# New job times and buffer letters for the first stage of a one-core S4 and gated-FFN kernel

## The chip, the core and the metric

One core of one Trainium2 chip runs the whole kernel. The metric is device microseconds (us) of one execution, the median of several runs. TensorE is PE in the profile (PEld its weight loads), VectorE is DVE, ScalarE is ACT, GpSimd is POOL, and SyncE is SP, which here only issues DMA transfers. "L843" is line 843 of the kernel.

## The reference

The input is `A_u`, 2048 tokens of 640 channels. A conditioning vector gives six rows that shift, scale and gate two residual blocks:

```python
mod = (_silu(c) @ w_mod).reshape(c.shape[0], 6, 1, -1)
sa, ca, ga, sb, cb, gb = (mod[:, 0], mod[:, 1], mod[:, 2], mod[:, 3], mod[:, 4], mod[:, 5])
h = _layernorm(x, axis=-1) * (1 + ca) + sa
x = x + ga * _A_ref(h, A_A_re, A_A_im, A_B_re, A_B_im, A_C_re, A_C_im, A_log_dt, A_Dskip)
h = _layernorm(x, axis=-1) * (1 + cb) + sb
x = x + gb * _B_ref(h, B_w_gate, B_w_up, B_w_down)
```

`_A_ref` builds for each channel a kernel of 2048 taps, `K = einsum("dn,dnl,dn->dl", Cc, exp(logdA * l), dB).real` over 192 complex modes, and convolves it with the tokens (written as an FFT of twice the length), plus a skip term. `_B_ref` is `((x w_gate) * (x w_up)) w_down` with 1536 hidden columns.

## The kernel before

The program has two stages. **The first stage** is block A. It works on five blocks of 128 channels (`db`) and interleaves two streams. One makes the taps K in 40 steps n of 16 channels each (8 steps a block): POOL multiplies out tables (`Ph`, `EQ`, `EP`, L732), ACT takes sines (tiles `tra`, `trb`), DVE multiplies both into the factors `QtA`, `PtA`, `QtB`, `PtB` (L787, L788, L793, L813), and PE sums them into the PSUM tile `kg`: 64 small matmuls at L828 (`kg_ma`, the A factors) and 64 at L843 (`kg_mb`, the B factors). ACT copies two steps' `kg` out as `Kt`. The other stream is the convolution by FFT, in jobs that are generators and advance one piece at a time: `u_k` (taps into the first FFT stage, PE L865), `u_pre` (tokens, PE L889), `u_g` and `u_c` (second stage, L913, product, and back, L973), and `u_d` (last stage, L996, and the residual, DVE L1002). `u_seeds` makes each block's seeds: PE transposes them at L538 to L540 into a PSUM bank, from which DVE reads several times, last at L609 into the tile `RH`. `u_stats` takes a tile's layer-norm statistics (DVE L487, L488).

The order on every engine's queue is that of one Python loop, which has 144 rounds t, three to a step n, each with two places `due(2 * t)` and `due(2 * t + 1)`. A table `SCHED` gives each piece of each job a number v; it runs at place `v // 10`, and within a place in the order of v. Negative numbers lie in the start, between pieces of the first seeds. Each engine works its queue strictly in that order. A second table, `SLOT`, gives the ring buffers: a string per ring, whose letters say which of two or three buffers the next tile takes. `psf` is a ring of three PSUM banks (`psfa`, `psfb`, `psfc`) that all the jobs share; a job that takes a bank waits until the last reader of that bank is done. `hf`, `gh`, `W`, `TV`, `xs` are rings in SBUF, in which loads also wait for the buffer's last reader.

```python
def due(x):
    for _, g in sorted(jobs.pop(x, []), key=lambda j: j[0]):
        next(g, None)
```

**The second stage** is block B in products of float32r halves; it starts at about 505 us (PE L1108) and its order is written out by hand.

The program is unrolled, so PE reads its instructions as a stream: its matmuls and weight loads come in by a DMA queue of their own ("q8 instruction" in the profile), in packets while it runs.

Of the kernel before, what the change touches and what calls it, by code (L numbers as in the profile page):

```python
# [69 lines left out]
    rstd=(142, 86),  # L70
    tab=(553, 739),
    fo=(149, 149, 202, 228),
    e0=(1, 159),
    ds=(339, 378, 319, 440),
    mc=((120, 175, 197, 201, 209), (192, 273, 273, 309, 317), (264, 369, 392)),
    q=(
# [4 lines left out]
    ),  # L81
    pre=(
# [5 lines left out]
    ),  # L88
    c=(
# [17 lines left out]
    ),  # L107
    k=(
        (402, 407),
        (224, 230),  # L110
        (454, 556),
        (421, 426),
        (484, 507),
        (517, 548),
        (639, 657),
        (603, 603),
        (706, 716),
        (664, 680),
        (777, 781),
        (803, 804),  # L120
        (1006, 1012),
        (1029, 1037),
        (1046, 1059),
        (1046, 1075),
        (1295, 1322),
        (1120, 1137),
        (1252, 1252),
        (1388, 1406),
        (1410, 1420),
        (1505, 1522),  # L130
        (1556, 1567),
        (1481, 1509),
        (1808, 1839),
        (1737, 1774),
        (1753, 1756),
        (1784, 1785),
        (1840, 1856),
        (1883, 1912),
        (1996, 2008),
        (2063, 2073),  # L140
        (2085, 2096),
        (2141, 2191),
        (2362, 2374),
        (2274, 2274),
        (2321, 2321),
        (2447, 2455),
        (2494, 2510),
        (2452, 2466),
    ),
    low=(167, 428, 668, 910, 1139, 1389, 1628, 1864, 2075),  # L150
    w=(2473, 2612, 2690, 2703, 2759, 2879),
    wl=(2602, 2481),
    wm=(2735, 2751),
    h=(2562, 2755, 2793, 2818, 2854, 2858, 2862, 2876),
    g=(
# [6 lines left out]
    xl=(2441, 2442),  # L162
# [3 lines left out]
    Kt="ababababababbabbaaba",  # L166
# [1743 lines left out]
```

## Time and profile before

| | |
|---|---|
| runs of before | 966.39, 969.98 and 972.0 us; median 969.98 |
| the profiled execution | 966.46 us, of which the span from first to last instruction is 964.6 |
| PE busy, 0 to 36 us | 17.7 of 36 (start) |
| PE busy, 36 to 505 us | 424.2 of 469 |
| PE busy, 505 us to the end | 455.4 of 459.6 (second stage) |
| transfers of PE's instructions | 91 packets, 1.49 MB |

An engine's idle time counts only where the others wait for it. A wait that the profile puts down to "issue" is one in which the engine waited for nothing that the profile shows as another engine or a data transfer.

### The profile page before, as it was taken

Reading aid. Unit: us, or ns where it says so; the run is one execution under the profiler, and the core shown is the slowest. Engines: PE = TensorE matmul, PEld = TensorE weight load, DVE = VectorE, ACT = ScalarE, POOL = GpSimd, SP = SyncE. Lnnn points to the kernel's source line nnn. Section 1 sums busy time; section 2 is a strip of 40 time slices with the busy share of each in tenths; the row PEclk is TensorE's granted clock in tenths of the full one; section 3 lists DMA queues with packets and bytes.
Section 4 is the critical chain, followed back from the end, with each engine's and each line's share of the span. In section 5 each row is a group of like instructions: output and inputs, shape, how many; then the busy total and the mean of one; then the engine's idle time right before and its main releaser. Section 6 shows DMA issues by size and latency. Waiting matters only on the chain.

```text
span 964.6 us, 27405 instructions
## 1 busy us (share of the span) xinstructions
PE 897.4 (93%) x11566; PEld 737.1 (76%) x11566; DVE 716.3 (74%) x1270; ACT 572.1 (59%) x996; POOL 471.1 (49%) x369
## 2 busy tenths in 40 slices
PE   2898888999899799999889999999999999999998
PEld 1675555788676478787648888889999788888998
DVE  8987898889889797876679555557575756578952
ACT  6899989787978868763356433344364543435430
POOL 3999996988499597650040445320113223231110
PEclk9997998999999799999999999999999999999999
DMA  7975674534376536457785675535546576758875
GB/s 237 333 235 174 198 224 157 169 110 149 88 218 188 145 92 193 131 189 249 248 268 197 211 245 161 196 137 151 192 150 190 156 245 213 247 164 290 246 242 191
DMA packets 156707, 188.56 MB, mean 195 GB/s; under 512 B 9764, under 2 KB 126376, under 8 KB 155432
## 3 DMA queue, kind: packets, MB, share of 16 engines
q1 hardware_dynamic: 147368, 155.47, 50.2%
q0 software_dynamic: 4752, 21.63, 7.7%
q10 hardware_dynamic: 4464, 9.70, 2.7%
q8 instruction: 91, 1.49, 0.7%
q14 instruction: 32, 0.26, 0.1%
HBM read 124.19 MB, written 62.59 MB: 194 GB/s over the span
## 4 chain that ended last, share of the span: by engine, by line
PE 70%; ACT 5%; DVE 5%; DMA 2%; issue 2%; POOL 0%; DVEq 0%; SPq 0%; POOLq 0%
PE pa L1108 20%; PE psg L1108 10%; PE pa L1545 7%; PE pa L1597 6%; PE kg L843 3%; PE psfc L973 3%; PE psfb L913 2%; PE kg L828 2%; PE psfb L973 2%; PE psfa L913 2%; PE psfc L913 2%; PE psg L1597 2%; PE psfc L889 1%; PE psfa L973 1%; PE psfb L889 1%
## 5 line engine op out<-in xcount | busy, mean ns | idle before, releaser
L1085 POOL TENSOR_TENSOR tf<-wur,wgb 128x256 f32<-128x256 f32 x23 | 17.6, 766 | 242.4 <-DVE wtl L1056 187.8
L732 POOL TENSOR_TENSOR EQ<-LQ,RH 128x1536 f32<-128x1536 f32 x40 | 114.7, 2867 | 10.7 <-DVE QtB L788 10.7
L1056 DVE TENSOR_TENSOR wtl<-tf,wth 128x256 fp32r<-128x256 f32 (+1 forms) x72 | 36.7, 512 | 59.1 <-ACT wth L237 59.1
L732 POOL TENSOR_TENSOR Phb<-LH,DH 128x1536 int32<-128x1536 int32 x21 | 59.6, 2837 | 39.0 <-ACT tra L237 32.6
L732 POOL TENSOR_TENSOR EP<-LP,RH 128x768 f32<-128x768 f32 x40 | 61.8, 1544 | 1.7 <-ACT RH L237 1.7
L1545 PE MATMUL pa<-wsg,sh 128*128 128x384 f32 (+1 forms) x304 | 58.1, 309 | 0.0
L732 POOL TENSOR_TENSOR Pha<-LH,DH 128x1536 int32<-128x1536 int32 (+1 forms) x20 | 54.0, 2702 | 5.3 <-ACT trb L237 4.4
L843 PEld LDWEIGHTS kg<-QtB,PtB 64*32 64x32 f32 x2560 | 39.6, 110 | 18.5 <-issue 13.4
L843 PE MATMUL kg<-QtB,PtB 64*32 64x64 f32 x2560 | 46.4, 222 | 6.0 <-issue 5.1
L1056 DVE TENSOR_TENSOR wsg<-wga,wsg 128x640 fp32r<-128x640 f32 x36 | 33.0, 918 | 17.0 <-ACT wsg L237 17.0
L1545 PEld LDWEIGHTS pa<-wsg,sh 128*128 128x128 f32 x304 | 45.4, 188 | 0.0
L1584 POOL DMA_DIRECT2D wsg<-wdc x21 | 11.2, 531 | 66.6 <-PE pa L1597 35.7
L237 ACT ACTIVATE sh<-a 128x512 fp32r<-128x512 f32 x55 | 33.3, 624 | 13.9 <-PE psg L1597 6.2
L237 ACT ACTIVATE wsg<-wga 128x640 fp32r<-128x640 f32 x36 | 26.3, 730 | 25.3 <-PE pa L1545 12.8
L1056 DVE TENSOR_TENSOR sl<-a,sh 128x512 fp32r<-128x512 f32 x55 | 38.0, 711 | 3.9 <-ACT sh L237 3.9
L1108 PE MATMUL pa<-hh,wsg 128*128 128x512 f32 x150 | 39.9, 393 | 0.0
L237 ACT ACTIVATE a<-pa 128x512 f32<-128x512 f32 x12 | 7.2, 596 | 49.5 <-PE pa L1108 49.5
L237 ACT ACTIVATE s<-pa 128x512 f32<-128x512 f32 x12 | 7.2, 598 | 47.9 <-PE pa L1108 47.9
L787 DVE TENSOR_TENSOR QtA<-trb,EQ 128x1024 f32<-128x1024 f32 x21 | 25.6, 1220 | 13.3 <-ACT trb L237 6.7
L237 ACT ACTIVATE wth<-tf 128x256 fp32r<-128x256 f32 (+1 forms) x72 | 32.4, 481 | 4.5 <-DVE tf L1086 1.8
L237 ACT ACT_TABLE_LOAD x25 | 32.1, 1283 | 4.4 <-DMA pta<-A_A_re 4.0
L1545 PE MATMUL pa<-wsg,sl 128*128 128x384 f32 (+1 forms) x152 | 34.5, 308 | 0.0
(647 smaller groups left out, 3216.6 us busy)
## 6 DMA issues: line engine op xcount, KB each, us to landing
wsg<-wdc POOLq DMA_DIRECT2D x21, 640.0 KB, 5.1
wgb<-B_w_gate SPq DMA_DIRECT2D x24, 320.0 KB, 3.3
wur<-B_w_up SPq DMA_DIRECT2D x24, 320.0 KB, 4.2
wsd<-wsg SPq DMA_DIRECT2D x12, 640.0 KB, 3.8
wga<-wdg SPq DMA_DIRECT2D x12, 640.0 KB, 5.4
wsg<-wsd POOLq DMA_DIRECT2D x12, 640.0 KB, 4.6
wdc<-xb SPq DMA_DIRECT2D x21, 320.0 KB, 6.5
TVa<-WD SPq DMA_DIRECT2D x20, 256.0 KB, 4.7
```

Source lines behind the costliest of these rows:

```text
L237: return S.activation(o, i, f, **kw)
L732: G.tensor_tensor(o.rearrange("p x (h l) -> p x h l", l=8), lo.unsqueeze(2).to_broadcast([P, rows, nh, 8]), hi.unsqueeze(3).to_broadcast([ ...
L787: return [lambda: V.tensor_tensor(Qt[:, :, :, 0:32], tr[:, :, :, ::-1], e[:, :, 0:32].unsqueeze(1).to_broadcast([P, 2, R, 32]), op=OP.mult ...
L828: PE.matmul(kg[j * 32 : j * 32 + 32, dd, :], PtA[:, c, dl * 4 + j, :], QtA[:, c, dl * 4 + j, :], start=dd == 0 and c == 0, stop=False, til ...
L843: PE.matmul(kg[j * 32 : j * 32 + 32, dd, :], PtB[lo : lo + 64, c, r, :], QtB[lo : lo + 64, c, r, :], start=False, stop=dd == 7 and c == 1, ...
L889: PE.matmul(r[c][o : o + 64], t_s1h[a, c] if i == 0 else t_one[a], h[a] if i == 0 else shr[a, d0].unsqueeze(1).to_broadcast([1, 4, P]), st ...
L913: PE.matmul(r[c][par * 64 : par * 64 + 64, i, :], t_tw[:, k0 + k, c, :], src[:, k, :], start=True, stop=True, tile_position=(0, par * 64))
L973: PE.matmul(r[par][:, i], t_ti[lo : lo + 64, qd * 4 + i, c, :], y[lo : lo + 64, i, :], start=k == 0, stop=k == len(x) - 1, tile_position=( ...
L1056: V.tensor_tensor(lo, v, hi, op=OP.subtract)
L1108: PE.matmul(ps, w[a][:, k], x[b][:, l], start=first and n == 0 and m == 0, stop=n == 2 and m == len(ks) - 1, skip_group_check=True)
L1545: PE.matmul(AC[tb][t][c], x[:, ts], w[:, cs], start=st, stop=f == NF - 1 and n == 2 and (c == 0 or t % 2 == 1))
L1597: PE.matmul(ps[t][:, :DC], AH[m][a][:, t * P : t * P + P], w[b], start=c == 0 and n == 0 and j in (0, 1, 3), stop=c == NH - 1 and n == 2, ...
```

## The change

Only numbers and letters in the two tables are new. The functions, the loop, the second stage and the number of matmuls, activations, vector operations and transfers are as before (on each engine the same instructions; the explicit semaphore waits between them differ by a few). Two lines of the diff stand for some 200:

```diff
-    ml=(38, 14, -923),
+    ml=(61, -905, -993),
...
-    psf="bacbaacbaacccabbcabcbacbbbcabcbcaabacabbbcbcbcabcaaacbbcbcabcababccabcabcacbacbbabacbacabcbabacbabcabcbbacbacbacbaccacba"
+    psf="cacbbcbbcbcabcabbcaabbabccbacabcbaccabababcacbcbabccabababcbcacabbcabcbacbacabbcbcabcbaacbacbacabbacbacbacbacbbcacbcbacb"
```

What it moves shows in the engines' orders. **First place**, some 310 us into the program of before, where the fourth block's seeds are made (n = 28 to 30). On PE, in before, from the second half of the transposes of seeds into `psfa` (`TVa`, `TVb` are loaded inputs of the last FFT stage, `Kta`, `Ktb` copied taps):

```order
L540 MATMUL psfa<-ct,prm 64x8x8
L996 MATMUL psfb<-TVa,ct 32x512 x4
L865 MATMUL psfa<-ct,Ktb 64x128 x8
L828 MATMUL kg<-QtA,PtAa 32x64 x32
L996 MATMUL psfc<-TVa,ct 32x512 x4
L996 MATMUL psfb<-TVb,ct 32x512 x4
L865 MATMUL psfc<-ct,Kta 64x128 x8
L843 MATMUL kg<-QtB,PtB 32x64 x32
```

and in the change:

```order
L540 MATMUL psfa<-ct,prm 64x8x8
L996 MATMUL psfb<-TVb,ct 32x512 x4
L996 MATMUL psfc<-TVa,ct 32x512 x4
L828 MATMUL kg<-QtA,PtAa 32x64 x32
L843 MATMUL kg<-QtB,PtB 32x64 x32
L865 MATMUL psfa<-ct,Ktb 64x128 x8
L913 MATMUL psfb<-f16b,t_tw 64x128 x2
```

The L865 that takes over bank `psfa` stood one row behind the L996 and now stands behind two of L996, L828 and L843; a third L996 has moved up to a place ahead of the L828 before these rows. On DVE at the same place, before, from the last cast of the seeds on:

```order
L598 CAST pta<-psfa 128x192
L1002 TENSOR_TENSOR xsa<-psfb,xsa 128x512
L609 TENSOR_TENSOR RH_153<-psfa,mults 128x1056
L609 TENSOR_TENSOR RH_151<-psfa,mults 128x1056
L619 TENSOR_SCALAR psfc<-ptb 128x192
```

and in the change:

```order
L598 CAST pta<-psfa 128x192
L813 TENSOR_TENSOR PtB<-trb,EP_142 128x512
L787 TENSOR_TENSOR QtB<-trb,EQ_140 128x16x32
L788 TENSOR_TENSOR QtB<-trb,EQ_140 128x16x32
L1002 TENSOR_TENSOR xsb<-psfb,xsb 128x512
L609 TENSOR_TENSOR RH_153<-psfa,mults 128x1056
L609 TENSOR_TENSOR RH_151<-psfa,mults 128x1056
L1002 TENSOR_TENSOR xsa<-psfc,xsa 128x512
L619 TENSOR_SCALAR psfb<-ptb 128x192
```

`PtB` and `QtB` of step n = 28, which L843 needs, now come ahead of both L609. On ACT at the same place, before, from the first sines of `trb` to the next `tra` (`RH`, `LQ`, `LP` are the seeds' exponentials):

```order
L237 ACTIVATE trb<-ab 128x512
L237 ACT_TABLE_LOAD
L237 ACTIVATE ptb<-ptb 128x192
...
L237 ACTIVATE RH_151<-RH_151 128x1056
L237 ACTIVATE PtAb<-Phb 128x1024
L237 ACT_TABLE_LOAD
L237 ACTIVATE tra<-Phb 128x512
L237 ACTIVATE tra<-PtAb 128x512
```

and in the change:

```order
L237 ACTIVATE trb<-ab 128x512
L237 ACTIVATE PtAb<-Phb 128x1024
L237 ACTIVATE tra<-Phb 128x512
L237 ACTIVATE tra<-PtAb 128x512
L237 ACT_TABLE_LOAD
L237 ACTIVATE ptb<-ptb 128x192
...
L237 ACTIVATE RH_151<-RH_151 128x1056
L237 ACT_TABLE_LOAD
L237 ACTIVATE trb<-Phb 128x512
L237 ACTIVATE trb<-PtAb 128x512
```

`PtAb` and both `tra` of step n = 29 have gone ahead of the six exponentials; `trb` stays behind them. On SP's queue, before, the transfers issued ahead of that place (`FH`, `WD`: intermediate FFT results in HBM; `gha`, `TVb`, `xsb` loads for later pieces):

```order
L900 DMA FH<-hfc 128x4x128
L903 DMA FH<-hfb 64x4x128 x2
L986 DMA TVb<-WD 128x4x128 x2
L991 DMA xsb<-A_u 128x4x128
L927 DMA gha<-FH 128x1024
L978 DMA WD<-Wa 128x1024
L900 DMA FH<-hfb 128x4x128
L903 DMA FH<-hfa 64x4x128 x2
```

and in the change:

```order
L900 DMA FH<-hfa 128x4x128
L903 DMA FH<-hfc 64x4x128 x2
L986 DMA TVb<-WD 128x4x128 x2
L991 DMA xsa<-A_u 128x4x128
L978 DMA WD<-Wb 128x1024
L900 DMA FH<-hfa 128x4x128
L903 DMA FH<-hfc 64x4x128 x2
L1008 DMA x2d<-xsa 128x4x128
```

The load of `gha` between the two groups of `FH` writes has gone to a later place. **Second place**, the start, on DVE at step n = 1 (`st` are layer-norm statistics of one tile), before:

```order
L1293 RECIPROCAL rs_94<-ry 128x10
L793 TENSOR_TENSOR PtAa<-trb,EP_143 128x1024
L487 BN_STATS st_533<-Wb 128x6 x2
L488 BN_AGGR mv_93<-st_533 128x2
L813 TENSOR_TENSOR PtB<-tra,EP_143 128x512
```

and in the change:

```order
L1293 RECIPROCAL rs_94<-ry 128x10
L487 BN_STATS st_501<-Wb 128x6 x2
L488 BN_AGGR mv_93<-st_501 128x2
L793 TENSOR_TENSOR PtAb<-trb,EP_143 128x1024
L487 BN_STATS st_506<-f16a 128x6 x2
L488 BN_AGGR mv_93<-st_506 128x2
L487 BN_STATS st_510<-f16a 128x6 x2
L488 BN_AGGR mv_93<-st_510 128x2
L487 BN_STATS st_534<-f16a 128x6 x2
L488 BN_AGGR mv_93<-st_534 128x2
L813 TENSOR_TENSOR PtB<-tra,EP_143 128x512
```

Four tiles' statistics now stand ahead of `PtB` of n = 1 where one did; before, the other three came right behind its `QtB`.

## Rows read from the trace of the kernel before

**Rows 1.** The page: busy time by engine, and PE's instruction queue (packets, MB, share).

```profile
PE 897.4 (93%) x11566; PEld 737.1 (76%) x11566; DVE 716.3 (74%) x1270; ACT 572.1 (59%) x996; POOL 471.1 (49%) x369
q8 instruction: 91, 1.49, 0.7%
```

**Rows 2.** Busy time by stretch: length, PE, PEld, DVE, ACT, POOL, clock, DMA share, GB/s.

```profile
60.00:160.00 100.00, 83.93 (x1762) 58.57 (x1762) 85.63 (x131) 92.69 (x156) 95.72 (x53) 0.92 0.66 215
160.00:310.00 150.00, 142.62 (x3342) 112.31 (x3343) 129.01 (x181) 121.80 (x206) 120.57 (x69) 0.98 0.48 143
310.00:335.00 25.00, 18.45 (x407) 13.22 (x406) 19.42 (x32) 20.45 (x31) 13.47 (x6) 0.80 0.51 149
335.00:441.00 106.00, 103.47 (x2584) 84.86 (x2582) 82.41 (x103) 75.35 (x131) 74.19 (x40) 1.00 0.53 160
```

**Rows 3.** PE's waits, 36 to 160 us: total, times, longest.

```profile
PE kg L843 <- issue: 2.2, 1, 2.2
...
PE psfb L865 <- issue: 1.0, 1, 1.0
...
PE psfc L390 <- issue: 0.8, 1, 0.8
```

**Rows 4.** PE's waits, 160 to 441 us.

```profile
PE psfa L865 <- DVE RH L609: 3.7, 1, 3.7
PE kg L843 <- issue: 2.8, 1, 2.8
PE kg L828 <- issue: 1.4, 2, 0.9
...
PE psfc L913 <- issue: 0.5, 1, 0.5
...
PE kg L832 <- issue: 0.4, 1, 0.4
```

**Rows 5.** Timeline of PE, 309 to 337 us: start, length, instruction, [idle before].

```profile
313.18 0.98 PE L843 MATMUL kg<-QtB,PtB 64*32 64x64 f32 x54
317.01 0.38 PE L843 MATMUL kg<-QtB,PtB 64*32 64x64 f32 x10 [2.85 <-issue]
...
318.68 1.93 PE L996 MATMUL psfb<-TVa,ct 64*32 64x512 f32 x8
...
335.50 1.10 PE L828 MATMUL kg<-QtA,PtAb 128*32 128x64 f32 x64 [0.23 <-DVE PtAb L793]
```

**Rows 6.** Queues at work from 310.3 to 314.4 us: packets, MB, share.

```profile
q1 hardware_dynamic: 718, 1.19, 90.5%
```

**Rows 7.** The same from 314.4 to 315.6 us.

```profile
q8 instruction: 1, 0.02, 4.9%
```

**Rows 8.** Transfers issued from 302 to 313 us: KB each, us to landing.

```profile
gha<-FH SPq DMA_DIRECT2D x1, 512.0 KB, 6.4
WD<-Wa SPq DMA_DIRECT2D x1, 512.0 KB
```

**Rows 9.** Timeline of DVE, 316 to 337 us.

```profile
318.80 0.37 DVE L595 CAST psfc<-psfa 128x192 int32<-128x192 f32 x1 [3.85 <-PE psfa L540]
...
334.22 1.22 DVE L793 TENSOR_TENSOR PtAb<-trb,EP 128x1024 f32<-128x1024 f32 x1
```

**Rows 10.** Timeline of ACT, 305 to 342 us.

```profile
317.42 0.60 ACT L237 ACTIVATE Kta<-kg 128x512 f32<-128x512 f32 x1 [3.26 <-PE kg L843]
...
323.04 0.85 ACT L237 ACTIVATE LQ<-RH 128x768 f32<-128x768 f32 x1 [0.18 <-DVE RH L609]
...
328.28 1.04 ACT L237 ACTIVATE PtAb<-Phb 128x1024 f32<-128x1024 int32 x1
329.32 1.28 ACT L237 ACT_TABLE_LOAD   x1
```

**Rows 11.** Timeline of DVE, 26 to 52 us.

```profile
46.55 0.88 DVE L487 BATCH_NORM_STATS2 st<-f16a 128x6 f32<-128x320 f32 x2
47.46 0.21 DVE L488 BATCH_NORM_AGGREGATE mv<-st 128x2 f32<-128x12 f32 x1
```

More of the change, by code (lines that the diff above doesn't have):

```diff
@@ L70 @@
[L70 to L75, printed above, removed]
-    q=(
[4 rows of a table removed]
+    ml=(61, -905, -993),
+    mr=(((112, 130), (132, 141)), ((52, 76), (98, 101)), ((-874, 29), (10, 34))),
+    st=(
+        (10, 91),
+        (-977, 91),
+        (100, 103),
+        (-979, 8),
+        (-1007, -862),
+        (21, 86),
+        (-1000, -933),
+        (-890, 18),
+        (-988, -896),
+        (-968, 1),
+        (-1010, -924),
+        (-993, -911),
+        (-978, -871),
+        (-878, 27),
+        (27, 64),
+        (-928, 4),
+    ),
@@ new lines @@
+    hm=(
+        (362, 402),
+        (-992, 437),
+        (133, 264),
+        (-1010, 375),
+        (-1004, 176),
+        (-972, 150),
+        (153, 188),
+        (99, 160),
+        (5, 105),
+        (167, 266),
+        (211, 311),
+        (141, 176),
+        (458, 500),
+        (415, 515),
+        (365, 513),
+        (246, 368),
+    ),
+    rstd=(128, 85),
+    tab=(351, 718),
+    fo=(149, 159, 195, 201),
+    e0=(5, 134),
+    ds=(393, 266, 388, 300),
+    mc=((100, 163, 181, 181, 225), (157, 249, 269, 301, 326), (240, 367, 391)),
@@ L101 @@
     d=(
[5 rows of a table removed]
-    ),
-    k=(
[L109 to L148, printed above, removed]
-    ),
@@ L150 @@
[L150 to L154, printed above, removed]
-    g=(
[5 rows of a table removed]
[5 rows of a table added]
+    ),
+    k=(
+        (338, 360),
+        (223, 257),
+        (520, 539),
+        (487, 587),
+        (557, 571),
+        (544, 573),
+        (585, 603),
+        (651, 651),
+        (666, 667),
+        (707, 707),
+        (881, 898),
+        (828, 841),
+        (884, 888),
+        (999, 1007),
+        (1055, 1055),
+        (1005, 1016),
+        (1255, 1256),
+        (1204, 1204),
+        (1265, 1298),
+        (1402, 1436),
+        (1389, 1413),
+        (1507, 1509),
+        (1565, 1572),
+        (1504, 1504),
+        (1801, 1814),
+        (1922, 1929),
+        (1784, 1792),
+        (1769, 1779),
+        (1857, 1857),
+        (1895, 1904),
+        (2022, 2032),
+        (2046, 2079),
+        (2181, 2212),
+        (2111, 2117),
+        (2374, 2380),
+        (2276, 2276),
+        (2344, 2367),
+        (2483, 2495),
+        (2461, 2461),
+        (2480, 2488),
+    ),
@@ L161 @@
+    low=(154, 439, 648, 902, 1122, 1371, 1582, 1859, 2113),
+    w=(2553, 2650, 2635, 2652, 2874, 2878),
+    wl=(2588, 2517),
+    wm=(2722, 2792),
+    h=(2678, 2696, 2788, 2805, 2818, 2828, 2854, 2872),
+    g=(
[5 rows of a table added]
     ),
-    xl=(2441, 2442),
+    xl=(2473, 2441),
 )
 SLOT = dict(
-    Kt="ababababababbabbaaba",
-    Ph="abababababababababababababababababababbb",
-    PtA="babaababababababababababababababaaababab",
-    TV="ababababaabababbaabbababbaaabbabbbbabaabababab",
-    W="baaabbaaabbabaabaaabbbaba",
@@ L171 @@
[L171 to L177 removed]
+    Kt="abababababababbababa",
@@ new lines @@
+    Ph="ababababababababababababababababababbaaa",
+    PtA="abaabaababababababaabbababababababababba",
+    TV="ababababaaabaabbabaabaabbaabbbbbaabaaaabbababa",
+    W="abbbbabababbbbaaaabaaabab",
+    f16="abababa",
+    gh="bcacbacbacbabcabcacbabcacbacabcabcabcab",
+    hf="cbcaacbcababccacbcaacacaacabbcbcacbcbcbacbabacaccabcabcbaaaccbacc",
+    psf="cacbbcbbcbcabcabbcaabbabccbacabcbaccabababcacbcbabccabababcbcacabbcabcbacbacabbcbcabcbaacbacbacabbacbacbacbacbbcacbcbacb"
+    "acacabcabcabcabbacbabcacbcababcabcabbcabcaabacbcbabcaabcabcbaacbacbaacbbccabacbbacbabacabcacbcbacbacbcabcaababcabcbacbca"
@@ L178 @@
+    "bcabcbacacbacbbacacbacabcbabcacbacba",
+    tr="ababababababababababababababababababababababababaabaabababaaababababbabbabababababababababababababaaabababababababbababa"
     "b",
-    xs="aabababbaabbaaab",
+    xs="abaabaabababaaab",
 )
```

46 lines of the change are left out of this document (4 added, 42 removed), and 46 rows, old and new, of tables (c, d, g, pre).

## The prediction

> **What bounds the kernel now.** I read the page first: PE is busy 93% of the span and each of the other engines less than 75% [rows 1], so the question is where PE's idle time in the first stage lies and what ends it. The second stage is the same in both programs and PE is busy 455.4 of its 459.6 us, so a change can come only from the 505 us ahead of it. The view by stretches divides these [rows 2]. From 60 to 160 us PE is busy 83.9 of 100, while POOL has 95.7 and ACT 92.7: here those two set the pace, and a pause of PE costs something only when it holds one of them up. From 160 to 310 us PE has 142.6 of 150 and from 335 to 441 us 103.5 of 106: here PE sets it, and a pause of PE is lost for good. Between lies the worst place of the first stage, 310 to 335 us, with PE at 18.4 of 25.
>
> PE's waits then tell which end last. Eight are put down to "issue": 2.2 + 1.0 + 0.8 = 4.0 us ahead of 160 us [rows 3], and 2.8 + 1.4 + 0.5 + 0.4 = 5.1 us in 160 to 441 us, next to the longest wait of all, 3.7 us of L865 for the seeds' last reader [rows 4]. What an "issue" wait is, the timeline shows at 314 us. Of the 64 matmuls of L843, 54 run, PE stops for 2.85 us, and 10 follow at 317.01 [rows 5]: a group of equal matmuls with all operands there breaks in its middle. PE has 2 x 11566 matmuls and weight loads in 91 packets, so 254 instructions a packet [rows 1]. In the 4.1 us up to the break (310.3 to 314.4) the queue of data transfers takes 90.5% of the DMA engines, and no packet of instructions moves [rows 6]; in the next 1.2 us one does [rows 7], and PE goes on 1.4 us after that window. So PE ran out of instructions behind data. Two of the transfers are 512 KB each, `gha` (6.4 us from issue to landing) and `WD` [rows 8].
>
> What the pause holds up: DVE stands 3.85 us for the transposes L540 behind it [rows 9] and ACT 3.26 us for `kg` [rows 10]. Then the chain of the seeds runs alone: DVE's casts from 318.80, both L609, ACT's exponentials from 323.04 (idle 0.18 for `RH`), then `PtAb`, a table load and the sines, and last DVE's `PtAb` L793, 334.22 + 1.22 = 335.44, for which PE waits 0.23 before 335.50.
>
> **The change, part by part.** *The place at 310 us.* The load of `gha` leaves the stretch ahead of the break. The queue moved 1.19 MB in 4.1 us [rows 6], that is 290 KB a us, so 512 KB fewer let PE's packet start up to 1.8 us sooner: the wait falls from 2.85 to about 1.05. Lower bound of the gain: nothing (what delays a packet may be another transfer, `WD` is still there); upper bound: the whole 2.85. I take 1.8, since the row that names the backlog is the one beside the break. Against it stands half an L996 that has moved up, four of eight matmuls at 1.93 us, so 1.0 us [rows 5]. Hence L540 ends about 0.8 us earlier than before.
>
> From there I walk the new order with the old durations. On DVE `PtB` and two `QtB` now stand ahead of L609, three operations that ran 0.6 us apart: +1.9 us. The exponentials thus start at 323.04 - 0.8 + 1.9 = 324.1. They take 5.2 (323.04 to 328.28 [rows 10]), to 329.4. `PtAb` and two sines of n = 29, which stood behind them, are now ahead, in the time in which ACT waited; left are the table load, 1.28, and two `trb` at 0.60, to 331.9; then L793, 1.22, ends at 333.1 against 335.44. **Term A = -2.3 us.** If the fetch wait stays 2.85 us it is -0.5; if the wait goes wholly, -3.4. The 3.7 us of L865 is no term of its own: L865 now stands behind L996, L828 and L843, which PE works while DVE is at the seeds, and that part of PE's time was spent waiting for the same chain. POOL, whose next `EQ` waits for `QtB` of n = 28, gets that sooner. From 335 to 441 us PE sets the pace, so A goes through.
>
> Here the Trainium skill speaks against the change. "Runtime: NRT & Kernel Launch", section "Instruction fetch mechanics", says that the sequencer brings blocks of 256 instructions in by its own queue while it runs the block before, and that crossing a block is mostly hidden. The trace agrees with the size of a block (254 instructions a packet) and disagrees on the hiding: 2.85 us in the middle of L843. By the page, less data ahead of a packet is worth nothing.
>
> *The other fetch waits.* With other instructions ahead of them the 254-instruction borders fall elsewhere. In 160 to 441 us the other waits are 5.1 - 2.85 = 2.3 us in four [rows 4]. A border costs much where PE runs through the block before it fast, as in dense groups of L828 and L843, and where the queue is full. Counting from the new order, the border that gave the 0.4 of L832 moves off, while two others fall behind denser rows, near 213 and 283 us, than any close to them before. So this term lies between -2.3 (all four go) and +1.8 (two new ones of 0.9, the longest of the L828 waits); I take **0**. Ahead of 160 us the waits of 4.0 us may go wholly, but POOL and ACT have only 4 and 7 us free in 100 there [rows 2], so PE's pauses lie beside their work: between -4.0 and 0, and I take **0**, nearer to the row of POOL. If that cover is gone, the 2.2 of L843 would count first.
>
> *The start.* `PtB` of n = 1 gets three statistics more ahead of it on DVE: 3 x (0.88 + 0.21) = 3.3 us [rows 11]. Queued behind them are `QtB`, for which POOL's next but one `EQ` waits, and L843 on PE. In before the same three follow right behind `QtB`, so DVE is even again a step later. Bounds 0 and +3.3; I take **0**, because the same 3.3 us only change places within one step. *The tail*, from 441 us, has almost the same order on PE and on the queues: 0.
>
> Sum: A -2.3, all others 0. The profiled execution of 966.46 us would come to 964.2. It lies 3.5 below the median of its runs, 969.98, so I set the change against the median: 969.98 - 2.3 = **967.7**, with its own bounds 964 to 971.
>
> **The rivals.** *The rule of the page, or: the change doesn't do what it says.* The fetch waits neither go nor come, or they move and add up to the same; the reorder at 310 us alone is left, with the wait at 2.85 us: -0.5, 969.5. For it: borders move with every edit, and 91 of them lie somewhere. Against it: `gha` is gone from just ahead of the costliest one. By the page it would come out so.
>
> *Faster: the fetch waits go as a whole.* A with no wait is -3.4, the four others -2.3, and the 2.2 of L843 ahead of 160 us, if POOL waits for what is behind it, -2.2: 969.98 - 7.9 = 962.1; with all of the 4.0, 960.3. For it: every one of the eight sits behind data on the queues or behind a dense block, which the placing of pieces can alter. Against it: the two new dense blocks, and ACT and POOL up to 160 us.
>
> *Slower: PE's clock.* PE's clock was 0.80 of full speed in 310 to 335 us, with PE idle 6.5 of 25, against 1.00 in the stretch behind it [rows 2]. At the lower level, 1.2 GHz, that is (1 - 0.80) x 2 x 25 = 10 us. So one long pause brings half speed for some 10 us, and matmuls then take twice as long (L828, 1.10 us when at full speed [rows 5]), which costs about 5 us where PE sets the pace. In 60 to 160 us it was 16 us and in 160 to 310 us 6 us by the same sum. If the new borders or the new bank letters make a pause of the like in 160 to 310 or 335 to 441 us, the time is 967.7 + 5 = 972.7, and with two, 977.7. For it: the whole order is new, and a new wait for a bank or for the border at 283 us is enough. Against it: PE's idle time in these stretches is small, 7.4 and 2.5 us, and consists of short waits. It decides from the point at which half speed in 160 to 441 us grows from 16 us by 15 or more.
>
> **How the numbers follow.** The measurement can tell some 0.5% of this kernel from no change: 965.1 and 974.8. The chances: forecast 0.38, the rule of the page or no effect 0.07, faster rival 0.35, slower 0.20. The forecast's own range gives 0.02 to "faster"; with the rivals that is faster 0.37, same 0.43, slower 0.20. The range goes from 957, below the faster rival with the scatter of the three runs (966.39 to 972.0), to 977.5, the slower rival with two pauses; it leaves out about 2 in 10.
>
> **What would show it.** Right: L843 and L538 of the fourth block's seeds follow each other with at most some 1 us between them; DVE's wait for L540 falls from 3.85 to about 2 or less; L865 no longer waits 3.7 us for `RH`; L793 `PtAb` of n = 29 ends 2 to 3 us earlier, and the second stage starts 2 to 3 us earlier, at about 502.5. The total of "issue" waits in 160 to 441 us stays above 2 us. Wrong: a break within L843 or L828 of 2 us or more at another place, a clock below 0.95 in a stretch that had 1.00, POOL or ACT idle more than 8 us in 60 to 160 us, or a first stage that ends after 505 us.

## The result, and the profile after

The change is slower: 974.17 us (median of 20 runs) against 969.86 us (20 runs of before), a ratio of 1.0043 with a 95% interval of 1.0026 to 1.0061, so 4.2 us. That is on the edge of what the prediction called telling from no change (0.5%), in the direction opposite to the forecast of 967.7, and inside its range. The profiled execution took 974.28 us, with a span of 972.5.

The page of the change, busy time by engine and PE's instruction queue, for [rows 1]:

```profile
PE 900.0 (93%) x11566; PEld 737.7 (76%) x11566; DVE 718.3 (74%) x1270; ACT 572.9 (59%) x996; POOL 472.8 (49%) x369
q8 instruction: 91, 1.49, 0.6%
```

The work is the same. Its busy time by stretch, columns as in [rows 2]:

```profile
60.00:160.00 100.00, 84.49 (x1787) 60.26 (x1787) 82.08 (x125) 88.58 (x149) 91.96 (x50) 0.89 0.64 210
160.00:310.00 150.00, 141.64 (x3327) 112.73 (x3325) 129.62 (x180) 122.91 (x206) 121.18 (x70) 0.97 0.46 136
310.00:335.00 25.00, 20.85 (x413) 12.47 (x411) 21.79 (x38) 21.63 (x34) 18.54 (x8) 0.93 0.73 203
335.00:441.00 106.00, 103.34 (x2538) 84.89 (x2536) 84.67 (x105) 78.57 (x135) 74.32 (x40) 1.00 0.51 156
```

In 60 to 160 us, PE is as busy as before, but POOL, which had 4.3 us free there, now has 8.0. All of PE's "issue" waits from 36 to 480 us, for [rows 3, 4]:

```profile
PE psfc L913 <- issue: 1.1, 1, 1.1
...
PE kg L843 <- issue: 0.3, 1, 0.3
...
PE psfa L889 <- issue: 0.2, 1, 0.2
```

They came to 9.1 us in before and come to 1.6 us here. So the waits for PE's instructions are nearly gone, and the kernel is slower all the same. Where PE stands in the two traces, worked out from its timelines (start of the group, us):

| PE begins | before | change | later by |
|---|---|---|---|
| L843 of n = 5 | 96.9 | 102.6 | 5.8 |
| L843 of n = 12 | 162.5 | 168.1 | 5.6 |
| L843 of n = 27 | 313.2 | 319.8 | 6.6 |
| L828 of n = 30 | 346.2 | 349.2 | 3.0 |
| L843 of n = 38 | 431.8 | 434.1 | 2.2 |
| L1108, first | 504.7 | 511.5 | 6.8 |

Three things happen: a loss of 5.8 us ahead of n = 5, a gain of 3.6 us at the place around 320 us, and a loss of 4.6 us between the end of the taps and the second stage.

**The first loss.** POOL's timeline in before (start, length, instruction, idle before), then that of the change:

```profile
86.99 2.86 POOL L732 TENSOR_TENSOR EQ<-LQ,RH 128x1536 f32<-128x1536 f32 x1
...
97.50 0.73 POOL L670 TENSOR_TENSOR D<-ptb 128x96 int32<-128x96 int32 x2 [3.15 <-issue]
...
102.79 2.83 POOL L732 TENSOR_TENSOR Pha<-LH,DH 128x1536 int32<-128x1536 int32 x1
```

```profile
95.07 2.87 POOL L732 TENSOR_TENSOR EQ<-LQ,RH 128x1536 f32<-128x1536 f32 x1 [3.42 <-DVE QtB L788]
...
103.25 0.74 POOL L670 TENSOR_TENSOR D<-ptb 128x96 int32<-128x96 int32 x2 [2.02 <-issue]
...
108.53 2.84 POOL L732 TENSOR_TENSOR Pha<-LH,DH 128x1536 int32<-128x1536 int32 x1
```

This `EQ`, which had no wait in before, now stands 3.42 us for DVE's `QtB` of n = 5. L670, the first POOL step on the second block's seeds, comes 5.75 us later; everything behind it keeps that distance (102.79 to 108.53). L670 reads what DVE's L665 casts, and the timeline of DVE in the change shows what L665 waited for:

```profile
90.42 0.17 DVE L464 TENSOR_SCALAR colT<-psfc 128x5 f32<-128x5 f32 x1 [0.95 <-PE psfc L461]
...
94.25 0.68 DVE L788 TENSOR_TENSOR QtB<-tra,EQ 128x512 f32<-128x512 f32 x1
...
102.76 0.36 DVE L665 TENSOR_SCALAR ptb<-psfb 128x192 int32<-128x192 f32 x1 [0.85 <-PE psfb L540]
```

and the timeline of PE, what was ahead of that L540:

```profile
83.90 0.49 PE L538 MATMUL psfb<-ct,prm 128*128 128x128 f32 x2 [1.96 <-ACT Wb L237]
...
88.10 2.29 PE L461 MATMUL psfc<-ident,Wb 1*128 1x1 f32 x10 [2.63 <-DVE ptb L597]
...
95.92 2.94 PE L438 MATMUL psfc<-t_ti,sil 128*128 128x320 f32 x10
98.69 2.85 PE L438 MATMUL psfa<-t_ti,sil 128*128 128x320 f32 x10
101.38 0.39 PE L538 MATMUL psfb<-ct,prm 128*128 128x128 f32 x2
...
101.96 0.49 PE L538 MATMUL psfb<-ct,pta 128*128 128x128 f32 x2
```

Two things hold POOL there. Its own queue is late at `EQ`, for which DVE's casts of the seeds and a wait for PE's L461 (the modulation's columns) come ahead of `QtB`: even without L665, POOL could not have begun L670 before 101.23 us, the end of the operation ahead of it, 3.7 us late. And L665 is 5.75 us later than in before. In before (timelines of DVE, of PE and of ACT):

```profile
97.01 0.36 DVE L665 TENSOR_SCALAR ptb<-psfa 128x192 int32<-128x192 f32 x1
```

```profile
93.62 2.86 PE L438 MATMUL psfc<-t_ti,sil 128*128 128x320 f32 x10
96.31 0.38 PE L538 MATMUL psfa<-ct,pta 128*128 128x128 f32 x2
```

```profile
94.51 0.35 ACT L237 ACTIVATE pta<-pta 128x192 f32<-128x192 f32 x1
```

The last transposes, those of `pta`, stood behind the 20 matmuls of L438 in before too (88.31 to 96.31 us). They read what ACT's arctangent writes into `pta`, and in the change that comes 6.18 us later (timeline of ACT):

```profile
100.69 0.35 ACT L237 ACTIVATE pta<-pta 128x192 f32<-128x192 f32 x1
```

It ends at 101.04, L438 at 101.54, so L438 can account for at most 0.5 of the 5.75 us. ACT has no wait ahead of its arctangent from 74 us on in either trace: the seeds' chain is late because ACT's queue is. At 70.47 us in the change (the copy `shr<-psfa`, 65.70 in before) ACT is already 4.8 us late, behind waits of 3.41 us for POOL's `EQ` and 2.10 us for PE's L415.

**The gain.** PE's timeline at the place of [rows 5]:

```profile
319.78 1.10 PE L843 MATMUL kg<-QtB,PtB 64*32 64x64 f32 x64
320.81 0.49 PE L538 MATMUL psfa<-ct,prm 128*128 128x128 f32 x2
...
332.43 1.09 PE L865 MATMUL psfa<-ct,Ktb 128*64 128x128 f32 x16
```

L843 is whole, the seeds' transposes follow at once, and this L865 no longer waits for `RH`.

**The second loss.** The chain that ended last, in the change (start, length, what):

```profile
475.42 7.43 DMA WD<-Wb
483.00 2.98 DMA TVa<-WD
486.03 1.96 PE psfa L996 x8
```

The last write of the FFT's intermediate result to HBM is issued at 475.42, and everything up to the second stage hangs on it. The same view of before has this write 5 us earlier:

```profile
470.44 6.42 DMA WD<-Wa
```

### The profile page after: what moved, and what is told of

Read it like the earlier page. It is cut to its first block, busy times and chain, and to the rows that moved or that the text cites. A ratio compares the mean times of both kernels' runs of the same rounds, so it can differ in the third digit from the quotient of the medians.

```text
span 972.5 us, 27385 instructions
## 1 busy us (share of the span) xinstructions
PE 900.0 (93%) x11566; PEld 737.7 (76%) x11566; DVE 718.3 (74%) x1270; ACT 572.9 (59%) x996; POOL 472.8 (49%) x369
## 4 chain that ended last, share of the span: by engine, by line
PE 40%; DVE 5%; DMA 3%; issue 3%; ACT 2%; POOL 0%; POOLq 0%; SPq 0%; ACTq 0%
PE pa L1108 20%; PE psg L1108 10%; PE pa L1545 7%; DMA WD<-Wb 1%; PE pa L1597 1%; DVE sl L1056 1%; DMA out<-wga 1%; DMA wsg<-wdc 1%; ACT hh L237 1%; DVE hl L1056 0%; PE psg L1199 0%; DVE e L1169 0%; DMA wga<-x2d 0%; DVE a L1578 0%; DVE wga L1612 0%
## 5 line engine op out<-in xcount | busy, mean ns | idle before, releaser
L732 POOL TENSOR_TENSOR Phb<-LH,DH 128x1536 int32<-128x1536 int32 x19 | 54.8, 2882 | 30.6 <-ACT tra L237 30.6
L732 POOL TENSOR_TENSOR Pha<-LH,DH 128x1536 int32<-128x1536 int32 (+1 forms) x22 | 59.9, 2721 | 12.8 <-ACT trb L237 8.4
L843 PEld LDWEIGHTS kg<-QtB,PtB 64*32 64x32 f32 x2560 | 39.8, 111 | 14.4 <-issue 9.1
L843 PE MATMUL kg<-QtB,PtB 64*32 64x64 f32 x2560 | 46.5, 224 | 1.4 <-DVE QtB L788 1.0
L1108 PE MATMUL pa<-hh,wsg 128*128 128x512 f32 x150 | 40.0, 393 | 0.0
L1545 PE MATMUL pa<-wsg,sl 128*128 128x384 f32 (+1 forms) x152 | 34.5, 308 | 0.0
L1108 PE MATMUL pa<-sh,wth 128*128 128x512 f32 x110 | 34.0, 391 | 0.4 <-ACT a L237 0.4
```

What stands on the lines that cost most here:

```text
L732: G.tensor_tensor(o.rearrange("p x (h l) -> p x h l", l=8), lo.unsqueeze(2).to_broadcast([P, rows, nh, 8]), hi.unsqueeze(3).to_broadcast([ ...
L843: PE.matmul(kg[j * 32 : j * 32 + 32, dd, :], PtB[lo : lo + 64, c, r, :], QtB[lo : lo + 64, c, r, :], start=False, stop=dd == 7 and c == 1, ...
L1108: PE.matmul(ps, w[a][:, k], x[b][:, l], start=first and n == 0 and m == 0, stop=n == 2 and m == len(ks) - 1, skip_group_check=True)
L1545: PE.matmul(AC[tb][t][c], x[:, ts], w[:, cs], start=st, stop=f == NF - 1 and n == 2 and (c == 0 or t % 2 == 1))
```

## The experiments

Each run is timed in five rounds beside before on the same chip; a ratio is to before, with its 95% interval. Nothing is left out of any kernel's work. Several are hybrids: the numbers v below a cut come from one table, those above from the other, and ring letters follow. A place at a cut that neither table has can cost time of its own. Cuts are given by the time in the program at which they fall.

**1. The noise.** The kernel before, under another name.

> The kernel before once more, with a profile of its own: its execution of 966.46 us was the lowest but one of its runs. All theories: ratio 1.000. The profile shows how much of the 7.9 us between the two profiled executions lies in the execution and not in the kernel: I expect 2 to 4 us, most of it in places where DMA transfers end a wait (the tail, and PE's fetches).

Measured: 969.09 us, 0.9979 [0.9956, 1.0002]. Its second profile (span 965.8) has other "issue" waits than the first, 4.8 us instead of 9.1:

```profile
PE kg L843 <- issue: 2.1, 3, 1.7
...
PE kg L832 <- issue: 1.1, 1, 1.1
```

So where a packet of instructions is late, and by how much, changes from one execution to the next of one program, and half of these waits can vanish with no time gained (spans of 964.6 and 965.8 us).

**2. Which part of the table.** `head_b`: numbers up to v = 540 (some 123 us) of before, the rest of the change. `head_a`: the reverse. `tail_b` and `tail_b2`: the change up to v = 2340 and 2420 (some 430 and 445 us), behind it before. `head_b24`: before only up to v = 240 (some 77 us). `best1`: the change only from v = 540 to 2420. `head_b` against the change, for example:

```diff
-    ml=(61, -905, -993),
+    ml=(38, 14, -923),
...
-    rstd=(128, 85),
+    rstd=(142, 86),
```

`head_b`, expected:

> The table of before up to place 54 (n = 9, about 123 us), the table of the change from there on; all work is done. Theory H (the loss comes in the first 120 us, where POOL fell 5.8 us behind and is then busy without a pause up to 160 us): the second stage starts about 5 us earlier than in the change, the time is about 969 us, ratio to before 0.999. Theory T (the loss is made behind 441 us alone, by an ACT write that waits 3.0 us for its buffer Wb): about 974, ratio 1.004. Theory N (many small losses, none of them decides): about 972.

`head_a`, expected:

> The table of the change up to place 54 (about 123 us), the table of before from there on; all work is done. Theory H: POOL is about 5.8 us late at n = 10 and the time is about 975, ratio 1.005 (up to 1 us less where before has slack behind 160 us). Theory T: about 970, ratio 1.000. Theory N: about 972.

`tail_b`, expected:

> The table of the change up to place 234 (n = 39, about 430 us), the table of before from there on; all work is done. Theory T: the wait of ACT for Wb goes and the second stage starts 3 us earlier, about 971, ratio 1.001. Theory H alone: about 974, ratio 1.004, the later start is carried through. If both are true: 971, and the rest of the loss shows in head_a.

`head_b24`, expected:

> The table of before up to place 24 (n = 4, about 77 us), the table of the change from there on; all work is done. Theory S: nearly the whole gain of head_b (4.7 us against the change) is there: 970, ratio 1.000. Theory M: little of it, 973 to 974, ratio 1.003.

`tail_b2`, expected:

> The table of the change up to place 242 (behind n = 40, about 445 us), the table of before from there on; all work is done. In tail_b the seam itself cost a wait of 2.5 us for f16b, so the seam stands later here. Theory T (the tail of the change costs 3 us, by the write into Wb that waits for its buffer and by the later product behind it): 971, ratio 1.001. Theory H alone (the tail is bound by what comes before it): 974, ratio 1.004.

`best1`, expected:

> The table of before up to place 54, that of the change from there to place 242, and that of before again behind it; all work is done. If the middle of the change gains 3.6 us at 310 us, as both the change and head_b show (PE 6.6 us late before, 3.0 behind; and 1.3 early before, 5.1 behind), and head and tail carry all the loss: 966, ratio 0.996. If the tail takes the gain back whatever its table: 970, ratio 1.000.

| kernel | first part | middle | tail | median us | ratio |
|---|---|---|---|---|---|
| the change | change | change | change | 974.17 | 1.0043 [1.0026, 1.0061] |
| head_b | before | change | change | 969.59 | 0.9995 [0.9968, 1.0022] |
| head_b24 | before to 77 us | change | change | 974.09 | 1.0039 [1.0019, 1.0058] |
| tail_b2 | change | change | before | 968.84 | 0.9983 [0.9959, 1.0007] |
| best1 | before | change | before | 964.21 | 0.9938 [0.9912, 0.9964] |
| tail_b | change | change | before from 430 us | 973.59 | 1.0025 [1.0002, 1.0048] |
| head_a | change | before | before | 986.97 | 1.0166 [1.0132, 1.0200] |

The change, `head_b`, `tail_b2` and `best1` fit a sum. The first part costs 1.0043 - 0.9995 = 0.48%, or by the other pair 0.9983 - 0.9938 = 0.45%: 4.4 to 4.7 us. The tail costs 0.60%, or by the other pair 0.57%: 5.5 to 5.8 us. The middle gains 0.62%, 6.0 us. Together 4.7 + 5.8 - 6.0 = 4.5, where 4.2 were measured. `best1` beats both kernels by some 0.6 and 1.0%. The two cuts that were misplaced tell less: in `tail_b` PE stands 2.49 us at the seam for `f16b`, and in `head_a` POOL is 12.3 us late at the `EQ` of 153.37 us (141.12 in before), more than in the change, so its seam adds. In `head_b24` the start is that of before, yet POOL's timeline shows the loss whole:

```profile
78.94 2.84 POOL L732 TENSOR_TENSOR Pha<-LH,DH 128x1536 int32<-128x1536 int32 x1 [1.30 <-ACT trb L237]
...
94.82 2.87 POOL L732 TENSOR_TENSOR EQ<-LQ,RH 128x1536 f32<-128x1536 f32 x1 [4.71 <-DVE QtB L788]
...
102.75 0.73 POOL L670 TENSOR_TENSOR D<-ptb 128x96 int32<-128x96 int32 x2 [1.77 <-issue]
```

So the pieces between the cuts at 77 and 123 us are enough to make the first part's loss. How the change itself comes to it isn't settled by that: at the copy `shr<-psfa`, where ACT is 4.8 us late in the change, it is 1.1 us late in `head_b24` (66.75), and only behind that copy does it become 5.7 us late, at the arctangent (100.17).

**3. Late statistics.** `stats_b`: seven statistics of the start, and one group of their square roots, back at before's numbers.

```diff
-        (10, 91),
-        (-977, 91),
+        (10, 115),
+        (-977, 121),
...
-    rstd=(128, 85),
+    rstd=(142, 85),
```

> The kernel of the change, in which only seven layer-norm statistics on DVE (and the second group's row statistics, which need them) stand behind PtA and PtB of n = 0 and n = 1 again, as in before; the orders of PE and SP are those of the change, all work is done. Theory S (these statistics make DVE late with QtB of n = 0 and 1, and with it POOL, which is then busy without a pause): QtB of n = 1 is done 3 us earlier, POOL's lag near 108 us falls from 5.7 to 2 or 3, the time is about 971, ratio to before 1.001. Theory M (POOL falls behind later, where the second block's seeds and the modulation stand between 75 and 95 us): 974, ratio 1.004.

Measured: 973.71 us, 1.0028 [1.0010, 1.0045]; POOL is 7.9 us late at the `EQ` of 129 us, not less than in the change. The statistics are not what makes POOL late, and the 0.15% by which the ratio lies below the change's is less than either interval.

**4. The chain L540, L665, L670.** `seeds_b` puts the second block's seeds (and the first two steps' taps) back at before's numbers. `mg_late` only moves L438 (all 20 matmuls) behind the seeds' second transposes; bank letters follow. `l609_late` moves only DVE: both L609 and L464 behind `QtB` of n = 5. `best2` is `best1` with L438 moved alike.

```diff
 seeds_b
-        (125, 174, 275, 300, 314, 322, 326, 348, 348, 360, 372, 375, 384, 501),
+        (176, 238, 239, 257, 257, 321, 321, 341, 341, 357, 366, 373, 378, 473),
 mg_late
-    mc=((100, 163, 181, 181, 225), (157, 249, 269, 301, 326), (240, 367, 391)),
+    mc=((100, 163, 181, 181, 225), (157, 249, 269, 301, 326), (240, 386, 391)),
 l609_late
-    mc=((100, 163, 181, 181, 225), (157, 249, 269, 301, 326), (240, 367, 391)),
+    mc=((100, 163, 181, 181, 225), (157, 249, 269, 301, 351), (240, 367, 391)),
-        (125, 174, 275, 300, 314, 322, 326, 348, 348, 360, 372, 375, 384, 501),
+        (125, 174, 275, 300, 314, 352, 353, 354, 355, 360, 372, 375, 384, 501),
```

`seeds_b`, expected:

> The kernel of the change, in which the second block's seeds (14 pieces) and the first two taps jobs stand where before has them; everything else is the change's, all work is done. Theory D (the head's 4.7 us come from these seeds: their casts stand between QtA and QtB of n = 5 on DVE, QtB of n = 5 comes late and POOL waits 3.4 us for it near 95 us, in a stretch in which POOL sets the pace): POOL's lag near 108 us falls from 5.7 to 2 or less, 970, ratio 1.000. Theory P (it is PE's waits for banks around the modulation, or several pieces together): 973 to 974, ratio 1.003 or more.

`mg_late`, expected:

> The kernel of the change, in which one piece alone stands two places later: the 20 matmuls of L438 (modulation, 5.6 us of PE near 96 us), behind the transposes L538 to L540 of the second block's seeds and the L843 of n = 5 instead of ahead of them; all other engines keep their order, all work is done. Theory C (the head's loss goes along the chain of the second block's seeds: PE reaches their second transposes late, DVE's L665 and with it POOL's L670 and all of POOL's work up to 160 us come late): L665 moves from 102.8 to 99 or 100, POOL's lag near 108 us falls by 3 us, 971, ratio 1.001. Theory Q (POOL is held by its wait of 3.4 us for QtB of n = 5 instead): L665 moves, the later POOL does not, 974, ratio 1.004.

`l609_late`, expected:

> The kernel of the change, in which DVE alone has another order at one place: both L609 of the second block's seeds (and L464) stand behind PtB and QtB of n = 5 instead of ahead of them; all work is done. Theory Q: QtB of n = 5 is done 3.6 us earlier, POOL's wait of 3.4 us at 95 us goes and POOL is 3 us earlier near 108 us, 971, ratio 1.001. Theory C: the wait goes, but POOL then waits as much longer for L665, which hangs on PE; no change, 974 to 975, ratio 1.004.

`best2`, expected:

> best1 with the L438 of the modulation behind the second transposes of the second block's seeds (in before PE works at L438 from 88.3 to 96.3 us, while the seeds' pta has been ready since 90.1). Theory C: L665 comes 4 to 6 us earlier, POOL's stretch up to 160 us with it, 960 to 961, ratio 0.990. Theory Q, or ACT is what comes next: as best1, 964, ratio 0.994.

All four are slower: 983.19 us, 1.0126 [1.0101, 1.0150]; 980.44 us, 1.0097 [1.0069, 1.0126]; 980.00 us, 1.0091 [1.0069, 1.0113]; and `best2` 971.12 us, 1.0009 [0.9987, 1.0031], where `best1` had 0.9938. All four hoped-for repairs failed; three of them show which link holds. In `l609_late` POOL's `EQ` waits less for `QtB`, as meant, but the bank that L609 reads comes free later. PE's timeline, DVE's and POOL's:

```profile
97.49 1.98 PE L865 MATMUL psfb<-ct,Kta 128*64 128x128 f32 x16 [4.57 <-DVE RH L609]
```

```profile
109.02 0.36 DVE L665 TENSOR_SCALAR ptb<-psfb 128x192 int32<-128x192 f32 x1 [1.53 <-PE psfb L540]
```

```profile
95.09 2.86 POOL L732 TENSOR_TENSOR EQ<-LQ,RH 128x1536 f32<-128x1536 f32 x1 [2.77 <-DVE QtB L788]
...
109.51 0.74 POOL L670 TENSOR_TENSOR D<-ptb 128x96 int32<-128x96 int32 x2 [8.26 <-issue]
```

L665 runs 6.26 us later than in the change (102.76), L670 6.26 us later (103.25), and the ratio is 0.48% higher, 4.7 us. `best2` shows what the last transposes wait for once L438 is out of their way (timeline of PE):

```profile
97.36 0.80 PE L538 MATMUL psfa<-ct,pta 128*128 128x128 f32 x2 [5.73 <-ACT pta L237]
```

Its expectation took `pta` as ready at 90.1 us in before, but that is DVE's part; ACT's arctangent ends at 94.86. In `mg_late` L665 runs at 100.93, but there all of this is 1.5 us ahead of the change before the moved piece comes (the first L538 at 82.40 instead of 83.90), so the move itself bought 0.3 us. L438's results then hold up ACT, 4.82 and 2.25 us on its copies of `Wb`, ahead of the sines, and POOL pays there (timeline):

```profile
111.06 2.84 POOL L732 TENSOR_TENSOR Pha<-LH,DH 128x1536 int32<-128x1536 int32 x1 [4.47 <-ACT trb L237]
```

In `seeds_b` L670 runs at 105.74, 2.5 us later still, and ahead of that POOL's `Ph` product waits 4.62 us for sines at 82 us; that run moves 18 numbers and doesn't single out one.

Across these kernels POOL's lateness passes into the time nearly one to one. How late the twelfth `EQ` is against before's 129.4 us, in one profile each, beside the ratio, for the kernels that share the change's middle and tail:

| | head_b | head_b24 | the change | stats_b | mg_late | l609_late | seeds_b |
|---|---|---|---|---|---|---|---|
| late by, us | 0.3 | 5.2 | 5.8 | 7.9 | 11.5 | 12.9 | 13.6 |
| ratio | 0.9995 | 1.0039 | 1.0043 | 1.0028 | 1.0097 | 1.0091 | 1.0126 |

From the first to the last, 13.3 us late cost 1.31%, 12.7 us. `best2` against `best1` says much the same: 8.9 us later, and 0.71%, 6.9 us. The lateness scatters: the seven other kernels with the change's order up to there had 5.8 to 8.2 where the change's profile had 5.8.

**5. The place at 310 us.** `gha_back`: in the change, the load of `gha` back to its place ahead of L843. `mid1500`: the change only from v = 1500 (some 291 us) to 2420.

```diff
-        ((1764, 1801, 1801), (1396, 1489, 1499), (1422, 1599, 1611), (1461, 1681, 1713)),
+        ((1664, 1801, 1801), (1396, 1489, 1499), (1422, 1599, 1611), (1461, 1681, 1713)),
```

`gha_back`, expected:

> The kernel of the change, in which one load of 512 KB (gha) is issued at about 313 us again, between the two groups of FH writes, as in before, instead of at 332 us; all work is done. Step A of the prediction (this load delays PE's instruction transfer by up to 1.8 us): PE stops for 1 to 2 us within L843 of n = 27, and what is behind it comes that much later, 975 to 976, ratio 1.006. Rival (the gain at this place comes from the order on DVE and ACT alone): no stop, 974, ratio 1.004.

`mid1500`, expected:

> The table of before up to place 150 (n = 25, about 293 us), that of the change from there to place 242, and that of before again; all work is done. It holds the place at 310 us but nothing of the change ahead of it. If that place carries the gain of the middle: the same as best1, 964 to 966, ratio 0.994 to 0.996. If the gain of best1 (6.0 us) comes mostly from 123 to 293 us: 968 to 969, ratio 0.998.

`gha_back`: 975.46 us, 1.0037 [1.0020, 1.0053], as the change. PE's timeline:

```profile
321.02 0.87 PE L843 MATMUL kg<-QtB,PtB 64*32 64x64 f32 x46
322.06 0.52 PE L843 MATMUL kg<-QtB,PtB 64*32 64x64 f32 x18 [0.17 <-issue]
```

With the 512 KB back in front of it, the packet of instructions moves later, but the stop is 0.17 us, not 2.85. From L843 of n = 27 to L828 of n = 30, PE took 33.0 us in before, 29.4 in the change, 29.7 in `gha_back` and 29.2 in `head_b`. So the place gains 3.3 us with `gha` where it was: in the new order the transfer makes hardly a stop, and nearly all of the gain is the order's, which includes that the stop is gone. That seems to be most of it: in the three profiles with before's order here (before, its repetition, `head_a`) the stop was 2.85, 1.69 and 2.52 us and the place took 33.0, 32.0 and 33.1; with the change's order it took 29.2 to 32.2 in 17 profiles, 29.5 in the middle one, so the gain is some 2.5 to 3.6 us. `mid1500` came to 971.03 us, 1.0003 [0.9981, 1.0024]: by its times this part alone brings nothing. Its profile has the gain at this place too (29.3 us), and loses more behind it, where PE stops three times for instructions, 6.1 us together. But that execution took 977.22 us, far above its median, so where in the middle the 6.0 us lie stays open beyond the some 3 at this place.

**6. The tail.** `w_b`: the change with the loads and splits of the second stage's first weights and tokens at before's numbers. `tail_j1`: the opposite, `tail_b2` with these loads where the change has them. `w_gh`: the change with the last `W` in a free buffer of the ring `gh`, which takes away ACT's wait of 2.96 us for `Wb`. `tw_d3`: the change with the fourth block's last pieces as before (the first at 2420 for 2410), and with them one job of the first block, whose pieces move by up to 24 numbers.

```diff
 w_b
-    w=(2553, 2650, 2635, 2652, 2874, 2878),
-    wl=(2588, 2517),
+    w=(2473, 2612, 2690, 2703, 2759, 2879),
+    wl=(2602, 2481),
 w_gh
-        W = ring(fp, [P, 4, 2, P], "W")
+        W = ring(fp, [P, 8, P], "gh").rearrange("p (i r) d -> p i r d", r=2) if (db, qd) == (NB - 1, 0) else ring(fp, [P, 4, 2, P], "W")
 tw_d3
-        ((2457, 2518, 2518), (2386, 2436, 2585), (2617, 2711, 2755), (2637, 2695, 2696)),
+        ((2420, 2495, 2559), (2386, 2438, 2661), (2692, 2692, 2730), (2651, 2688, 2715)),
```

`w_b`, expected:

> The kernel of the change, in which only the loads of the second stage's first weights and tokens behind 440 us (two loads of 640 KB that are issued between the last writes of WD, and those of the tokens) and their splits stand as in before; all work is done. Theory W (these loads share the queues with the last two writes of WD, which makes ACT wait 3 us for Wb and the last write take 7.4 us): the last write ends 2 to 4 us earlier, 971, ratio 1.001. Theory O (the order of the products and of the buffers W makes it): 974, ratio 1.004.

`w_gh`, expected:

> The kernel of the change, in which the last of the twenty products W of the first stage is put into a buffer of gh that is free by then, instead of Wb; orders are the same, all work is done. Theory B (the tail's 5.8 us come from ACT's wait of 3.0 us for Wb, and what follows from it): the wait goes, the last write of WD is issued 3 us earlier, 970 to 971, ratio 1.001. Theory O (the order of products and transfers there makes it; the earlier write only takes longer): 973 to 974, ratio 1.004.

`tail_j1`, expected:

> After up to some 445 us; behind that the jobs of before (last pieces of the FFT stages, head of the second stage), but the loads of weights and tokens (w, wl, xl) where the change has them. All work is done. If the place of these loads is what costs the tail its 5 us (theory L: they lie on the queues in front of the last W writes), this stays near 974, ratio 1.004. If the order of the jobs is the cause (theory J), it comes to 968 to 970, ratio 0.998 to 1.000, and the last W write is issued some 4 to 5 us earlier against L843 of n = 39 than in the change.

`tw_d3`, expected:

> The change with only the last pieces of the fourth block (u_d: loads of TV, L996, residual) back at the numbers of before, some later, some earlier; two letters of the TV ring follow. All work is done. If these pieces, taken earlier in the change, are what delays the last u_c pieces on PE and the queues (one form of theory J), 969 to 971; if it is the last block's own pieces (the other form), it stays at 973 to 976.

Measured: `w_b` 976.90 us, 1.0064 [1.0040, 1.0088]; `w_gh` 973.29 us, 1.0024 [1.0004, 1.0044]; `tail_j1` 971.46 us, 1.0019 [0.9997, 1.0040]; `tw_d3` 983.52 us, 1.0134 [1.0115, 1.0153]. The wait for the buffer is worth 0.19%, 1.8 us, if the two ratios are taken at their middles: `w_gh` issues its last write at 474.33 instead of 475.42, where `tail_b2` has it at 470.73. The chain that ended last in `tail_b2`:

```profile
470.73 6.58 DMA WD<-Wa
477.46 3.00 DMA TVb<-WD
```

Jobs and loads depend on each other: with the jobs of before, the change's loads cost 1.0019 - 0.9983 = 0.36%; with the change's jobs, before's loads make it 0.21% slower, not faster (the intervals overlap in both pairs). `tw_d3` shows how a single job out of step is paid for, in PE's waits:

```profile
PE psfb L996 <- DMA TVa<-WD: 6.0, 1, 6.0
```

That the tail costs 5.5 to 5.8 us is shown; that a third of it is the buffer is only as sure as the two overlapping intervals, and the rest is not taken apart further.

## Why the prediction was wrong, step by step

**The step that failed first** is "Ahead of 160 us the waits of 4.0 us may go wholly, but POOL and ACT have only 4 and 7 us free in 100 there [...]: between -4.0 and 0, and I take 0". It saw rightly that POOL sets the pace, and then costed only the removal of PE's waits, as if nothing that the table moves could make POOL itself late. In before the seeds of the second block reached POOL with 3.15 us of waiting, which is in the timeline of POOL above; every microsecond more that L540 and L665 take is added to POOL's 95.7 busy of 100. The chain was 5.75 us later, mostly through ACT, whose arctangent of the seeds came 6.18 us later, and the first part cost 4.4 to 4.7 us. Which pieces of the table make ACT late stays open: none of the four edits brought the time back. The prediction listed "POOL or ACT idle more than 8 us in 60 to 160 us" as a sign of being wrong; POOL's idle time is 8.0 there and ACT's 11.4. But no rival carried that mechanism or its price.

**The second** is "the tail, from 441 us, has almost the same order on PE and on the queues: 0". Almost the same order cost 5.5 to 5.8 us by the times (3.6 us in the pair of profiles, from L843 of n = 39 to L1108: 505.70 - 441.05 = 64.7 in `tail_b2`, 511.52 - 443.25 = 68.3 in the change). There one write and one read through HBM follow each other, 7.43 and 2.98 us in the change, and the second stage hangs on them.

**Term A**, -2.3 us, was right in sign, and what came is nearest to its case "if the wait goes wholly, -3.4": the place gained 3.6 us in this pair (33.0 to 29.4). Its signs at the place appeared: L843 and L538 follow each other, DVE's wait for L540 fell from 3.85 to 0.74 us, L865 no longer waits. Its later signs did not: L793 of n = 29 ended at 338.22 instead of before's 335.44, since all of it came 6.6 us late, the second stage began at 511.5, and the "issue" waits in 160 to 441 us fell to 1.4, below 2. The reason given for 1.8 of it, 512 KB less ahead of PE's packet, fell with `gha_back`, which gained 3.3 us with the load in its old place. The prediction's lower case, "if the fetch wait stays", was costed on a stop that belongs to the old order.

**The other fetch waits**, taken at 0 within -2.3 to +1.8, went almost wholly: 9.1 to 1.6 us in this pair. That was the mechanism of the rival "faster", with 0.35 of the chance, and it bought nothing that shows: `best1`, the fastest kernel, has 7.1 us of them in its profile (PE's waits):

```profile
PE psfc L913 <- issue: 3.1, 2, 2.0
...
PE kg L843 <- issue: 2.3, 1, 2.3
...
PE kg L828 <- issue: 1.7, 1, 1.7
```

and the change, with 1.6 us, is 10 us slower. The same holds of one order: `head_b` has the change's order from 123 us on, and its L828 stops for 2.49 and 1.82 us at 434 and 421 us, where the change's runs through. The Trainium skill, "Runtime: NRT & Kernel Launch", section "Instruction fetch mechanics", says that crossing a block of instructions is mostly hidden. The profiles of before disagree (2.85 us within L843), while the times agree in part with what follows from it: the sum of such stops in a trace said little about the time, though the one within L843 seems to have cost what it lasted.

**The start** at 0 was right: `head_b24` took the start of before and kept the loss.

**The rival "slower"**, half speed of PE's clock, was not the cause. By the prediction's own sum (the mean granted clock by stretch) half speed took 16, 6, 10 and 0 us in the four stretches of before, and (1 - 0.89) x 2 x 100 = 22, 9, 3.5 and 0 in the change: 32 us against 34.5, and the increase lies where POOL sets the pace; in 160 to 441 us, where the rival looked for it, the sum fell from 16 to 12.5. So the time fell on the slower rival's side by another road.

**The range**, 957.0 to 977.5, held the time, since it was opened on the upper side for that rival.

## What to carry to other kernels

Where two engines set the pace, cost a new order by what reaches *them*, not by the pauses it takes from a third: follow each chain of short steps (here arctangent, transposes, cast, table) that feeds the pacing engine, and ask what was put ahead of each link and which of two waits ends last: L438 stood ahead of the transposes, but they hung on ACT. A reshuffled table is a sum of parts with either sign; cut it at places in time and time the halves, since "same" or a small loss may hide 6 us gained and 10 lost, and the good part can be kept (here 964.21 us). A wait that scatters between two profiles of the same program is not a term of a sum until a second profile repeats it.

## What the runs showed of the chip beyond that

One DVE operation took three times its time. The timeline of DVE in the change:

```profile
28.48 3.39 DVE L630 TENSOR_TENSOR LQ<-LQ,LQ 128x768 f32<-128x768 f32 x1
```

The nine other L630 of that trace took 0.90 to 0.95 us, and the same one took 1.10 in before. In the change it began beside POOL's `EQ` (28.20 to 31.06), and it ended 0.8 us after it; POOL's next step took 3.56 us instead of 2.83. In before the POOL step beside it, a pair of L702, took 2.11 instead of 1.52. The Trainium skill, "SBUF — State Buffer", section "SBUF: two separate sides", says that DVE and POOL share a pair of ports that one of them holds for a whole instruction, when the DVE operation has two inputs in SBUF and the POOL operation reads there. The trace agrees with it as far as it goes: this L630 is the only one of the ten with both inputs in SBUF (`LQ`, `LQ`). The nine others read one input from a PSUM tile, and so do the 80 L787 (`tra` and `trb` lie in PSUM), of which more than 50 in each trace ran wholly beside POOL products in their usual 0.68 or 1.23 us. It is one operation a trace, and no run varied it.
